# Four output banks, low parts last, and the sums of w_out made early: a change to an attention and cosine-FFN kernel

## The chip, the cores and the metric

The kernel runs on one core of a Trainium2 chip. The metric is the device time of one execution in microseconds (us). The names of engines are those of the profile: PE is TensorE (matmuls; PEld its weight loads), DVE is VectorE, ACT is ScalarE, POOL is GpSimd, SP is SyncE, which issues the transfers. SBUF is the memory on the chip that all engines work from, PSUM the one that PE writes its results to (eight banks of 128 x 512 fp32 values), HBM the memory outside.

## The reference

```python
B, H, S, D = q.shape                       # 8, 8, 576, 64
scores = scale * np.matmul(q, k.transpose(0, 1, 3, 2))
# heads 0-3: the last 32 positions; heads 4-7: every 32nd position
scores = np.where(masks[None], scores, -1e9)
attn = softmax(scores)
x = matmul(attn, v).transpose(0, 2, 1, 3).reshape(B * S, H * D)   # 4608 x 512
h = x @ w_in                               # 512 x 2048
g = h * np.cos(h)
return g @ w_out                           # 2048 x 512
```

## The kernel before, in words

All products of the FFN are made from split operands: a value is the sum of a high part `hi` (rounded to the form that PE multiplies at full rate) and a low part `lo`, and one product takes three matmuls, hi·hi, hi·lo and lo·hi. `split` makes the two parts: a cast (L172, on ACT unless told otherwise) and a subtraction (L173, on POOL unless told otherwise).

**Stage 1** (to about 491 us) runs over 8 batches. For each it makes the attention of the next batch and `h` of this one, in 8 column tiles f of 7 slots each (a batch is 56 slots, `PER_BATCH`; `STEP` is 7). `Block.product` (L524) makes one of seven products of a 2x2 scheme, which needs seven block products in place of eight; `SLOTS` says in which slots they stand. h goes to HBM (`h_all`). Beside the products a plan of slots puts in other work step by step (`in_steps`): the preparation of `w_in`, of `w_out` (`whole_output_weights`, written to `w_all` in HBM in the middle batches; `output_weights` loads and splits a row block n of 16, twelve in the last batch and the last `LATE` = 4 in stage 2), and of sums of blocks of `w_out` that the 2x2 scheme needs (`output_sums`: three sets, for f in `SEVEN` = 1, 3, 5; the sums are made on DVE in the last batch and split there).

**Stage 2** runs over 18 token blocks s (256 tokens) and, in each, over 8 tiles f (two row blocks of w_out, so 256 of the 2048 columns of h). `gate(s, f)` makes g of one tile in steps, and `ahead` issues these steps 6, 4, 3 and 2 tiles before the tile's matmuls (`LEADS`):

- load `h_in` from HBM (L623, five buffers),
- `r`: an int32 rounding of h/2π on ACT (L630), then r = h − 2π·k on DVE (L631, a SCALAR_TENSOR_TENSOR, "stt"; three buffers),
- `wave`: the sine on ACT (L634) into one of three PSUM banks of the pool `sg`,
- in plain tiles: wave·h on DVE (L641), cast to `g_hi` on ACT (L172), `g_lo` by L173, on DVE for f = 2 and 4 (`BY_VECTOR`) and on POOL for 0, 6 and 7,
- in "seven" tiles (f = 1, 3, 5 of the blocks 1 to 16): wave·h into `g` on DVE (L648), three sums on POOL (L649, L650, L653), the cast of 128 x 896 on ACT, and `g_lo` of 128 x 896 on POOL. `g_hi` and `g_lo` have three buffers.

`Outputs.pair` makes the matmuls of a tile (L681): a plain tile takes 12 of 512 columns, a seven tile 21 of 256 columns. They add up in PSUM over the eight tiles of a block in the banks "lower" and "upper" (rows 0 to 127 and 128 to 255 of the block; one pool of three banks) and, for products that both halves share, "more" (two banks). `shared` adds the "more" parts up after f = 5 (ACT L706; DVE L707, L709, L712), and `store` adds them to both halves (DVE L721, twice), or, in blocks 0 and 17, which have no seven tiles, copies them (ACT L727, DVE L725), and stores the rows (L728). PSUM in stage 2 is thus 3 banks of wave, 3 of lower/upper and 2 of "more".

The order of the instructions on each engine isn't the order of the code. A scheduler sets it before the run from a timeline of its own (`schedule_with_timeline_sim=True`); only the matmuls keep the written order (`in_turn`). Any edit in buffers or engines may change the order on ACT, DVE and POOL.

Of the kernel before, what the change touches and what calls it, by code (L numbers as in the profile page):

```python
# [13 lines left out]
F32 = mybir.dt.float32  # L14
# [68 lines left out]

BY_VECTOR = (2, 4)

SUMMED = (14, 28, 35)
LATE = 4

OUTPUTS = (
    (0, "b11", "more", 0), (2, "b21", "upper", 0), (6, "b22", "upper", 1), (1, 3, "lower", 0), (5, 2, "more", 1),  # L90
# [5 lines left out]
def attention_cos_ffn(ctx, tc, qkl, vl, qkvs, w_in, w_out, eye, eye16, mask_l0, mask_l, mask_s, out):  # L96
# [74 lines left out]
    def split(x, hi, lo, cast=nc.scalar.copy, rest=nc.gpsimd):  # L171
        with_product(cast(out=hi, in_=x))  # L172
        rest.tensor_tensor(out=lo, in0=x, in1=hi.bitcast(F32), op=ALU.subtract)  # L173
# [401 lines left out]
        nc.sync.dma_start(out=w_all[n], in_=t)  # L575
        yield

    def output_weights(both, n):
        t = wp.tile([P, 2, 2, 2 * P], F32R, name="w", bufs=2 * NF).rearrange("p l m n -> p l (m n)")
        nc.sync.dma_start(out=both, in_=w_all[n])  # L580
        yield
        split(both, t[:, 0], t[:, 1], nc.vector.tensor_copy)
        wo.append((t[:, 0], t[:, 1]))
        yield

    def whole_tile(cv):
        return cv.tile([P, 512, 2], I32, name="raw", bufs=3).bitcast(F32).rearrange("p n w -> p (n w)")

    def output_sums(cv, n):

        f = SEVEN[n]
        both = whole_tile(cv).rearrange("p (f n) -> p f n", f=2)
        nc.sync.dma_start(out=both, in_=w_all[2 * f:2 * f + 2].rearrange("f p n -> p f n"))
        yield
        b = both.rearrange("p f (j n) -> p (f j) n", j=2)
        t = whole_tile(cv).rearrange("p (j n) -> p j n", j=4)
        first = nc.vector.tensor_tensor(
            out=t[:, :2], in0=b[:, 1:2].broadcast_to([P, 2, 2 * P]), in1=b[:, 0:4:3], op=ALU.subtract
        )
        with_product(first)  # L600
        nc.vector.tensor_tensor(out=t[:, 2], in0=b[:, 3], in1=t[:, 0], op=ALU.subtract)
        nc.vector.tensor_tensor(out=t[:, 3], in0=b[:, 2], in1=t[:, 2], op=ALU.subtract)
        most = wp.tile([P, 2, 3, 2 * P], F32R, name="v")
        sums[f] = [(most[:, 0, n], most[:, 1, n]) for n in range(3)]
        yield
        split(t[:, :3], most[:, 0], most[:, 1], nc.vector.tensor_copy)
        yield
        if n % 3 == 0:
            lasts.append(wp.tile([P, 2, 3, 2 * P], F32R, name="v"))
        last = lasts[-1][:, 0, n % 3], lasts[-1][:, 1, n % 3]  # L610
        split(t[:, 3], *last, nc.vector.tensor_copy)
        sums[f].append(last)
        yield

    wo, lasts, gates, sums = [], [], {}, {}
# [1 line left out]
    def seven(s, f):  # L617
        return 0 < s < NTB - 1 and f in SEVEN
# [49 lines left out]
    class Outputs:  # L668


        def __init__(self, s):
            self.s, self.banks, self.begun = s, {}, set()

        def add(self, name, begin, end, pairs):
            if name not in self.banks:
                n = 4 if name == "more" else 2
                self.banks[name] = pools[name].tile([P, n, 2 * P], F32, name="q")
            at = self.banks[name][:, begin:end].rearrange("p n d -> p (n d)")
            bank = name, begin // 2
            for a, w in pairs:  # L680
                in_turn(nc.tensor.matmul(  # L681
                    at, a, w, start=bank not in self.begun, stop=True, skip_group_check=True
                ))
                self.begun.add(bank)

        def pair(self, f, g_hi, g_lo):
            (b1h, b1l), (b2h, b2l) = wo[2 * f:2 * f + 2]
            if not seven(self.s, f):
                for half, name in enumerate(("lower", "upper")):
                    for n, (wh, wl) in enumerate(((b1h, b1l), (b2h, b2l))):  # L690
                        gh, gl = (g[:, (2 * n + half) * P:(2 * n + half + 1) * P] for g in (g_hi, g_lo))
                        self.add(name, 0, 2, ((gh, wh), (gh, wl), (gl, wh)))
                return
            left, right = slice(0, 2 * P), slice(2 * P, 4 * P)
            plain = {"b11": (b1h[:, left], b1l[:, left]), "b21": (b2h[:, left], b2l[:, left]),
                     "b22": (b2h[:, right], b2l[:, right])}
            for n, w, name, at in OUTPUTS:
                wh, wl = plain[w] if w in plain else sums[f][w]
                gh, gl = (g[:, n * P:(n + 1) * P] for g in (g_hi, g_lo))
                self.add(name, at, at + 1, ((gh, wh), (gh, wl), (gl, wh)))  # L700

        def shared(self):

# [11 lines left out]
        def store(self):  # L715

            rows = out[self.s * TB:(self.s + 1) * TB, :].rearrange("(h p) d -> h p d", h=2)
            for half, name in enumerate(("lower", "upper")):
                o = op.tile([P, 2, 2 * P], F32, name="o", bufs=4)
                if "more" in self.banks:  # L720
                    nc.vector.tensor_tensor(  # L721
                        out=o, in0=self.banks[name], in1=self.t[:, 2 - 2 * half:4 - 2 * half], op=ALU.add
                    )
                elif half:
                    nc.vector.tensor_copy(out=o, in_=self.banks[name])  # L725
                else:
                    nc.scalar.copy(out=o, in_=self.banks[name])  # L727
                nc.sync.dma_start(out=rows[half], in_=o.rearrange("p n d -> p (n d)"))  # L728

# [3 lines left out]
    with ExitStack() as phase:  # L733
# [67 lines left out]
                plan[STEP * f + slot] = partial(first.products, slot)  # L801
        for i, (b, f) in enumerate(itertools.product(range(1, B), range(NF)), NF):
            block = Block(b, f)
            for n, slot in enumerate(SLOTS):
                plan[STEP * i + slot] = partial(block.product, n)
        steps = {}

        def in_steps(work, *slots):
            work = iter(work)
            for slot in slots:  # L810
                steps.setdefault(slot, []).append(partial(next, work, None))
# [9 lines left out]
            in_steps(whole_output_weights(cv, n), at - 10, at)  # L821
        for n in range(NFC - LATE):
            at = (B - 1) * PER_BATCH + STEP * (n // 2) + 12 + 3 * (n % 2)
            in_steps(output_weights(whole_tile(cv)[:, :DM], n), at - 6, at)
        for n, at in enumerate(SUMMED):
            at += (B - 1) * PER_BATCH
            in_steps(output_sums(cv, n), at - 8, at, at + 2, at + 7)
# [36 lines left out]
    pools = {  # L864
        name: ctx.enter_context(
            tc.tile_pool(name=f"ps_{bufs}", bufs=bufs, space=bass.MemoryType.PSUM, reuse_waits="tile")
        ) for name, bufs in (("lower", 3), ("more", 1))
    }
    pools["upper"] = pools["lower"]
    made = {}  # L870
    for n in range(NFC - LATE, NFC):
        weights = output_weights(tp.tile([P, DM], F32, name=f"both{n}"), n)
        next(weights)
        made[n + LATE - NFC + 1] = [weights]
    for i, (s, f) in enumerate(tiles):
        if f == 0:
            block = Outputs(s)
# [105 lines left out]
```

## Time and profile before

| | |
|---|---|
| median of 3 runs | 891.18 us (890.71 to 891.97) |
| the profiled execution | 893.41 us, of which the span of the profile 891.6 us |
| mean granted clock of PE | 0.996 |
| PE busy | 867.6 us, 97% |
| DVE, ACT, POOL busy | 611.6, 506.3, 516.3 us |
| stage 2 | 18 blocks from 491.1 us on; last matmul ends at 887.7 us |

The profile shows one execution by instruction. A row of the timeline has the start, the duration, the engine, the line of the code, the operation, output <- inputs, the shape, a count, and in brackets how long the engine stood idle before it and what released it. A row of the costliest groups has busy time, mean ns of one, then idle time before them and its releaser. Durations in the sums below are those of the profiled execution; what is worked out in them is set against its own time.

### The profile page before, as it was taken

What the parts mean: (1) busy time and instruction counts of PE and PEld (TensorE: products, weight loads), DVE (VectorE), ACT (ScalarE), POOL (GpSimd) and SP (SyncE); (2) the same over time, 40 slices, a digit from 0 to 9 for tenths busy, and PEclk for the clock granted to TensorE, in tenths of its full rate; (3) what the DMA queues carried; (4) which work ended last, traced back from release to release, by engine and by line L of the source; (5) the groups of instructions that cost most, each with busy time, mean ns of one, the idle gap of its engine ahead of it and who ended that gap; (6) DMA issues with size and microseconds to landing.
All of it is one profiled execution on the core that took longest, in us unless ns stands there. A gap on an engine that the chain in (4) does not pass through costs nothing.

```text
span 891.6 us, 22375 instructions
## 1 busy us (share of the span) xinstructions
PE 867.6 (97%) x8871; PEld 788.7 (88%) x8871; DVE 611.6 (69%) x1097; ACT 506.3 (57%) x1004; POOL 516.3 (58%) x455
## 2 busy tenths in 40 slices
PE   8999999999999999999998999999999999999998
PEld 5799899999999998999998888888888888888886
DVE  5688656766676575575459777777777777777772
ACT  4666444435444463453425676666666666666672
POOL 3578974316024151150456787777777777777752
PEclk9899999999999999999999999999999999999999
DMA  9588444565556556544376533344343444433330
GB/s 330 187 286 277 135 150 157 193 224 190 196 185 229 187 196 212 193 162 169 111 233 207 162 115 119 122 124 123 122 123 121 122 123 124 123 124 119 119 99 31
DMA packets 89768, 145.46 MB, mean 163 GB/s; under 512 B 8256, under 2 KB 52544, under 8 KB 89664
## 3 DMA queue, kind: packets, MB, share of 16 engines
q1 hardware_dynamic: 88944, 143.82, 49.5%
q8 instruction: 69, 1.13, 0.5%
q14 instruction: 35, 0.29, 0.1%
q10 hardware_dynamic: 720, 0.23, 0.1%
HBM read 92.63 MB, written 51.38 MB: 162 GB/s over the span
## 4 chain that ended last, share of the span: by engine, by line
PE 37%; DVE 9%; issue 4%; ACT 3%; POOL 3%; POOLq 0%; DVEq 0%
PE q L681 28%; PE m L524 5%; DVE r L631 3%; POOL g_lo L173 3%; PE n L524 3%; ACT r L630 2%; PE o L524 1%; DVE t L709 1%; DVE o L721 1%; ACT wave L634 1%; DVE g L648 1%; DVE t L707 1%; DVE t L712 1%; DVE h L542 0%; PE acc L325 0%
## 5 line engine op out<-in xcount | busy, mean ns | idle before, releaser
L681 PE MATMUL q<-w,g_hi 128*128 128x512 f32 (+1 forms) x1056 | 293.4, 363 | 8.1 <-DVE o L721 8.1
L681 PEld LDWEIGHTS q<-w,g_hi 128*128 128x128 f32 x1056 | 187.6, 189 | 44.9 <-DVE o L721 14.8
L681 PE MATMUL q<-w,g_lo 128*128 128x512 f32 (+1 forms) x528 | 190.3, 360 | 0.0
L631 DVE SCALAR_TENSOR_TENSOR r<-r,h_in 128x512 f32<-128x512 int32 x144 | 144.0, 1019 | 9.8 <-ACT r L630 9.8
L173 POOL TENSOR_TENSOR g_lo<-g,g_hi 128x896 fp32r<-128x896 f32 x48 | 102.1, 2127 | 41.7 <-ACT g_hi L172 41.7
L634 ACT ACTIVATE wave<-r,quarter 128x512 f32<-128x512 f32 x144 | 98.2, 690 | 40.0 <-DVE r L631 40.0
L681 PEld LDWEIGHTS q<-w,g_lo 128*128 128x128 f32 x528 | 99.5, 188 | 15.8 <-POOL g_lo L173 0.2
L524 PE MATMUL m<-x_hi,w 128*128 128x288 f32 x448 | 109.9, 300 | 3.0 <-DVE h L542 2.6
L524 PE MATMUL m<-x_hi,v 128*128 128x288 f32 x448 | 109.0, 298 | 1.2 <-ACT m L532 1.2
L173 POOL TENSOR_TENSOR g_lo<-r,g_hi 128x512 fp32r<-128x512 f32 x60 | 85.8, 1431 | 35.8 <-ACT g_hi L172 34.5
L630 ACT ACTIVATE r<-h_in 128x512 int32<-128x512 f32 x144 | 86.4, 623 | 13.0 <-POOL g_lo L173 12.4
L172 ACT CAST g_hi<-g 128x896 fp32r<-128x896 f32 x48 | 45.3, 944 | 68.8 <-POOL g L653 68.8
L524 PEld LDWEIGHTS m<-x_hi,w 128*128 128x128 f32 x448 | 78.0, 188 | 5.2 <-DVE h L542 3.6
L532 ACT COPY m<-m 128x288 f32<-128x288 f32 x112 | 44.6, 399 | 63.4 <-PE m L524 57.9
L524 PEld LDWEIGHTS m<-x_hi,v 128*128 128x128 f32 x448 | 78.0, 188 | 2.5 <-ACT m L532 1.6
L277 POOL TENSOR_TENSOR pn_s<-e_sb,z 128x324 f32<-128x324 f32 x28 | 21.2, 758 | 94.1 <-DVE z L275 76.3
L277 POOL TENSOR_TENSOR e_sb<-e_sb,z 128x384 f32<-128x384 f32 x24 | 21.0, 873 | 92.6 <-DVE z L275 83.5
L681 PE MATMUL q<-v,g_hi 128*128 128x256 f32 x384 | 71.2, 283 | 0.0
L641 DVE TENSOR_TENSOR r<-wave,h_in 128x512 f32<-128x512 f32 x60 | 41.1, 686 | 39.4 <-ACT wave L634 39.4
L524 PE MATMUL m<-x_lo,w 128*128 128x288 f32 x224 | 66.1, 295 | 0.0
L524 PE MATMUL m<-x_lo,v 128*128 128x288 f32 x224 | 66.1, 295 | 0.0
L648 DVE TENSOR_TENSOR g<-wave,h_in 128x512 f32<-128x512 f32 x48 | 33.1, 689 | 42.3 <-ACT wave L634 42.3
(134 smaller groups left out, 2086.8 us busy)
## 6 DMA issues: line engine op xcount, KB each, us to landing
h_all<-h SPq DMA_DIRECT2D x128, 288.0 KB, 2.7
h_in<-h_all SPq DMA_DIRECT2D x144, 256.0 KB, 2.8
out<-o SPq DMA_DIRECT2D x36, 256.0 KB, 2.1
qk<-in_qkvs SPq DMA_DIRECT2D x28, 324.0 KB, 4.2
qk<-in_qkl SPq DMA_DIRECT2D x21, 416.0 KB, 4.0
raw<-in_w_in SPq DMA_DIRECT2D x16, 512.0 KB, 5.0
raw<-in_w_out SPq DMA_DIRECT2D x16, 512.0 KB, 4.3
v<-in_vl SPq DMA_DIRECT2D x24, 224.0 KB, 3.8
```

The costliest lines, as they stand in the source:

```text
L172: with_product(cast(out=hi, in_=x))
L173: rest.tensor_tensor(out=lo, in0=x, in1=hi.bitcast(F32), op=ALU.subtract)
L277: nc.gpsimd.tensor_tensor(out=pn, in0=e, in1=z[:, :n].unsqueeze(2).broadcast_to([P, n, w]), op=ALU.mult)
L524: in_turn(nc.tensor.matmul(bank, a[:, c * P:(c + 1) * P], y[:, c], start=first and i == 0, stop=i == len(ops) - 1, skip_group_check=True,))
L532: nc.scalar.copy(out=t, in_=self.bank[name[0]])
L630: with_product(nc.scalar.activation(out=k, in_=h, func=AF.Copy, scale=1.0 / (2.0 * math.pi), bias=0.25))
L631: nc.vector.scalar_tensor_tensor(out=r, in0=k, scalar=-2.0 * math.pi, in1=h, op0=ALU.mult, op1=ALU.add)
L634: sin = nc.scalar.activation(out=wave, in_=r, func=AF.Sin, bias=quarter)
L641: nc.vector.tensor_tensor(out=low, in0=wave, in1=h, op=ALU.mult)
L648: nc.vector.tensor_tensor(out=g[:, :4].rearrange("p n t -> p (n t)"), in0=wave, in1=h, op=ALU.mult)
L681: in_turn(nc.tensor.matmul(at, a, w, start=bank not in self.begun, stop=True, skip_group_check=True))
L707: nc.vector.tensor_tensor(out=self.t[:, 4], in0=more[:, 1], in1=self.t[:, 0], op=ALU.add)
```

## The change

1. PSUM: "lower" and "upper" share four banks instead of three; `wave` has two instead of three.
2. `Outputs.pair` issues, for a tile, first all matmuls with the high part of g and then all with its low part. In the very last tile the products of the upper half are made in two halves of 256 columns, and `store` copies and stores that half in two parts.
3. `output_sums` moves from the last batch to the middle batches (slots 2·56 + 17·(2f + 2) and 8 later), from DVE to POOL, and stores its sums in a new HBM tensor `t_all`. `split_sums` loads a set and splits it: two sets in the last batch, the third in tiles 6 and 7 of stage 2; their casts are on ACT and not on DVE.
4. `output_weights`: the casts of the ten row blocks in the last batch are on ACT and not on DVE; six row blocks instead of four are prepared in stage 2 (`LATE`), their casts on ACT and DVE in turn.
5. The very last tile of stage 1 has the seven products in other slots (`LAST`).

```diff
+LAST = (0, 4, 2, 3, 7, 6, 8)
...
-SUMMED = (14, 28, 35)
-LATE = 4
+SUMMED = (14, 28)
+LATE = 6
...
+    t_all = dram.tile([len(SEVEN), P, 2 * DM], F32, name="t_all")
...
-    def output_weights(both, n):
+    def output_weights(room, n, cast):
+        both = room()
...
-        split(both, t[:, 0], t[:, 1], nc.vector.tensor_copy)
+        split(both, t[:, 0], t[:, 1], cast)
...
-        first = nc.vector.tensor_tensor(
+        with_product(nc.gpsimd.tensor_tensor(
             out=t[:, :2], in0=b[:, 1:2].broadcast_to([P, 2, 2 * P]), in1=b[:, 0:4:3], op=ALU.subtract
-        )
-        with_product(first)
-        nc.vector.tensor_tensor(out=t[:, 2], in0=b[:, 3], in1=t[:, 0], op=ALU.subtract)
-        nc.vector.tensor_tensor(out=t[:, 3], in0=b[:, 2], in1=t[:, 2], op=ALU.subtract)
+        ))
+        nc.gpsimd.tensor_tensor(out=t[:, 2], in0=b[:, 3], in1=t[:, 0], op=ALU.subtract)
+        nc.gpsimd.tensor_tensor(out=t[:, 3], in0=b[:, 2], in1=t[:, 2], op=ALU.subtract)
+        nc.sync.dma_start(out=t_all[n], in_=t.rearrange("p j n -> p (j n)"))
+        yield
+
+    def split_sums(room, n):
+        t = room()
+        nc.sync.dma_start(out=t, in_=t_all[n])
+        yield
+        t = t.rearrange("p (j n) -> p j n", j=4)
         most = wp.tile([P, 2, 3, 2 * P], F32R, name="v")
...
-        split(t[:, :3], most[:, 0], most[:, 1], nc.vector.tensor_copy)
+        split(t[:, :3], most[:, 0], most[:, 1])
...
-            for a, w in pairs:
-                in_turn(nc.tensor.matmul(
-                    at, a, w, start=bank not in self.begun, stop=True, skip_group_check=True
-                ))
-                self.begun.add(bank)
...
+            for group in groups:
+                for n, both, to in group:
+                    for w in both:
+                        self.add(*to, g_hi[:, n * P:(n + 1) * P], w)
+                for n, (w, _), to in group:
+                    self.add(*to, g_lo[:, n * P:(n + 1) * P], w)
...
+                parts = (slice(0, 1), slice(1, 2)) if self.last and half else (slice(0, 2),)
+                for i, part in enumerate(parts):
+                    if "more" not in self.banks:
+                        copy = nc.scalar.copy if half == i else nc.vector.tensor_copy
+                        copy(out=o[:, part], in_=self.banks[name][:, part])
...
-                        name="sg", bufs=3, space=bass.MemoryType.PSUM, side="right", reuse_waits="tile"
+                        name="sg", bufs=2, space=bass.MemoryType.PSUM, side="right", reuse_waits="tile"
...
-        ) for name, bufs in (("lower", 3), ("more", 1))
+        ) for name, bufs in (("lower", 4), ("more", 1))
```

In the new file the lines of the gate are: r L642 (was L630), stt L643 (L631), sine L646 (L634), wave·h L653 (L641) and L660 (L648), POOL's three sums L661, L662, L665 (L649, L650, L653), cast L176 (L172), subtraction L177 (L173), matmul L692 (L681), `shared` L728 to L734 (L706 to L712), the two sums of `store` L743 (L721).

The edits also give another order on the engines of the gate. On POOL, one steady block (token block 6; `g` is a seven tile's, in turn f = 1, 3, 5; `g_lo<-r` is the low part of a plain tile, f = 6, 7 of block 5 and then f = 0), before:

```order
L173 TENSOR_TENSOR g_lo_9251<-g_9228,g_hi_9250 128x896
L173 TENSOR_TENSOR g_lo_9284<-r_9233,g_hi_9283 128x512
L173 TENSOR_TENSOR g_lo_9308<-r_9257,g_hi_9307 128x512
L649 TENSOR_TENSOR g_9349<-g_9349 128x128
L650 TENSOR_TENSOR g_9349<-g_9349 128x256
L173 TENSOR_TENSOR g_lo_9344<-r_9290,g_hi_9343 128x512
L653 TENSOR_TENSOR g_9349<-g_9349 128x128
L649 TENSOR_TENSOR g_9409<-g_9409 128x128
L173 TENSOR_TENSOR g_lo_9374<-g_9349,g_hi_9373 128x896
L650 TENSOR_TENSOR g_9409<-g_9409 128x256
L653 TENSOR_TENSOR g_9409<-g_9409 128x128
L173 TENSOR_TENSOR g_lo_9434<-g_9409,g_hi_9433 128x896
```

The same place after, from the low part of f = 0 on (the three low parts ahead of it stand as before):

```order
L177 TENSOR_TENSOR g_lo_9354<-r_9300,g_hi_9353 128x512
L661 TENSOR_TENSOR g_9359<-g_9359 128x128
L662 TENSOR_TENSOR g_9359<-g_9359 128x256
L665 TENSOR_TENSOR g_9359<-g_9359 128x128
L177 TENSOR_TENSOR g_lo_9384<-g_9359,g_hi_9383 128x896
L661 TENSOR_TENSOR g_9419<-g_9419 128x128
L662 TENSOR_TENSOR g_9419<-g_9419 128x256
L665 TENSOR_TENSOR g_9419<-g_9419 128x128
L661 TENSOR_TENSOR g_9483<-g_9483 128x128
L177 TENSOR_TENSOR g_lo_9444<-g_9419,g_hi_9443 128x896
L662 TENSOR_TENSOR g_9483<-g_9483 128x256
L665 TENSOR_TENSOR g_9483<-g_9483 128x128
```

The low part of f = 0 now stands ahead of all three sums of f = 1 (before, behind the second), and the first sum of f = 5 (L661, `g_9483`) ahead of the low part of f = 3 (before, behind it).

On DVE in the same block, from the stt of f = 1 on, before:

```order
L631 SCALAR_TENSOR_TENSOR r_9314<-r_9314,h_in_9260 128x512
L648 TENSOR_TENSOR g_9349<-wave_9347,h_in_9260 128x512
L631 SCALAR_TENSOR_TENSOR r_9354<-r_9354,h_in_9293 128x512
L631 SCALAR_TENSOR_TENSOR r_9380<-r_9380,h_in_9317 128x512
...
L631 SCALAR_TENSOR_TENSOR r_9414<-r_9414,h_in_9357 128x512
L721 TENSOR_TENSOR o_9397<-q_9174,t_9340 128x512
L721 TENSOR_TENSOR o_9400<-q_9181,t_9340 128x512
L173 TENSOR_TENSOR g_lo_9404<-wave_9377,g_hi_9403 128x512
L641 TENSOR_TENSOR wave_9437<-wave_9437,h_in_9357 128x512
L631 SCALAR_TENSOR_TENSOR r_9440<-r_9440,h_in_9383 128x512
L648 TENSOR_TENSOR g_9473<-wave_9471,h_in_9383 128x512
```

And after:

```order
L643 SCALAR_TENSOR_TENSOR r_9324<-r_9324,h_in_9270 128x512
L643 SCALAR_TENSOR_TENSOR r_9364<-r_9364,h_in_9303 128x512
L660 TENSOR_TENSOR g_9359<-wave_9357,h_in_9270 128x512
...
L643 SCALAR_TENSOR_TENSOR r_9450<-r_9450,h_in_9393 128x512
L743 TENSOR_TENSOR o_9407<-q_9184,t_9350 128x512
L743 TENSOR_TENSOR o_9410<-q_9189,t_9350 128x512
L177 TENSOR_TENSOR g_lo_9414<-wave_9387,g_hi_9413 128x512
L653 TENSOR_TENSOR wave_9447<-wave_9447,h_in_9367 128x512
L643 SCALAR_TENSOR_TENSOR r_9488<-r_9488,h_in_9427 128x512
L660 TENSOR_TENSOR g_9483<-wave_9481,h_in_9393 128x512
```

The stt of f = 2 (`r_9364`) moved ahead of the product of f = 1 (L660), and the stt of f = 5 (`r_9450`) ahead of the two sums of `store`; that of f = 6 (`r_9488`) ahead of the product of f = 5.

On PE, the tile f = 0 of block 6 (two weights each for the lower and the upper bank), before and after:

```order
L681 MATMUL q_9419<-w_7380,g_hi_9343 128x512 x2
L681 MATMUL q_9419<-w_7380,g_lo_9344 128x512
L681 MATMUL q_9419<-w_7410,g_hi_9343 128x512 x2
L681 MATMUL q_9419<-w_7410,g_lo_9344 128x512
L681 MATMUL q_9426<-w_7380,g_hi_9343 128x512 x2
L681 MATMUL q_9426<-w_7380,g_lo_9344 128x512
```
```order
L692 MATMUL q_9429<-w_7391,g_hi_9353 128x512 x2
L692 MATMUL q_9429<-w_7422,g_hi_9353 128x512 x2
L692 MATMUL q_9434<-w_7391,g_hi_9353 128x512 x2
L692 MATMUL q_9434<-w_7422,g_hi_9353 128x512 x2
L692 MATMUL q_9429<-w_7391,g_lo_9354 128x512
L692 MATMUL q_9429<-w_7422,g_lo_9354 128x512
```

The first use of the low part moved from the third matmul to the ninth.

More of the change, by code (lines that the diff above doesn't have):

```diff
@@ L596, in output_sums @@
         t = whole_tile(cv).rearrange("p (j n) -> p j n", j=4)
-        first = nc.vector.tensor_tensor(
+        with_product(nc.gpsimd.tensor_tensor(
             out=t[:, :2], in0=b[:, 1:2].broadcast_to([P, 2, 2 * P]), in1=b[:, 0:4:3], op=ALU.subtract
-        )
-        with_product(first)
-        nc.vector.tensor_tensor(out=t[:, 2], in0=b[:, 3], in1=t[:, 0], op=ALU.subtract)
-        nc.vector.tensor_tensor(out=t[:, 3], in0=b[:, 2], in1=t[:, 2], op=ALU.subtract)
+        ))
[8 more added lines that the diff above has]
+        t = t.rearrange("p (j n) -> p j n", j=4)
         most = wp.tile([P, 2, 3, 2 * P], F32R, name="v")
-        sums[f] = [(most[:, 0, n], most[:, 1, n]) for n in range(3)]
-        yield
-        split(t[:, :3], most[:, 0], most[:, 1], nc.vector.tensor_copy)
+        split(t[:, :3], most[:, 0], most[:, 1])
+        sums[SEVEN[n]] = [(most[:, 0, n], most[:, 1, n]) for n in range(3)]
         yield
@@ L610, in output_sums @@
         last = lasts[-1][:, 0, n % 3], lasts[-1][:, 1, n % 3]
-        split(t[:, 3], *last, nc.vector.tensor_copy)
-        sums[f].append(last)
+        split(t[:, 3], *last)
+        sums[SEVEN[n]].append(last)
         yield
@@ L671, in __init__, with add @@
         def __init__(self, s):
-            self.s, self.banks, self.begun = s, {}, set()
-        def add(self, name, begin, end, pairs):
+            self.s, self.banks, self.begun, self.last = s, {}, set(), s == NTB - 1
+        def add(self, name, begin, end, a, w):
             if name not in self.banks:
@@ L679, in add @@
             bank = name, begin // 2
-            for a, w in pairs:
-                in_turn(nc.tensor.matmul(
-                    at, a, w, start=bank not in self.begun, stop=True, skip_group_check=True
-                ))
-                self.begun.add(bank)
-        def pair(self, f, g_hi, g_lo):
[L687 to L700, printed above, removed]
@@ new lines, in add @@
+            in_turn(nc.tensor.matmul(at, a, w, start=bank not in self.begun, stop=True, skip_group_check=True))
+            self.begun.add(bank)
+        def pair(self, f, g_hi, g_lo):
+            w1, w2 = wo[2 * f:2 * f + 2]
+            if seven(self.s, f):
+                left, right = slice(0, 2 * P), slice(2 * P, 4 * P)
+                plain = {name: [w[:, part] for w in both] for name, both, part in (
+                    ("b11", w1, left), ("b21", w2, left), ("b22", w2, right),
+                )}
+                products = [
+                    (n, plain[w] if w in plain else sums[f][w], (name, at, at + 1)) for n, w, name, at in OUTPUTS
+                ]
+            else:
+                products = [
+                    (2 * n + half, w, (name, 0, 2)) for half, name in enumerate(("lower", "upper"))
+                    for n, w in enumerate((w1, w2))
+                ]
+            groups = [products]
+            if self.last and f == NF - 1:
+                groups = [products[:2], *(
+                    [(n, [w[:, 2 * P * i:2 * P * (i + 1)] for w in both], ("upper", i, i + 1))
+                     for n, both, _ in products[2:]] for i in range(2)
+                )]
+            for group in groups:
[4 more added lines that the diff above has]
+                    self.add(*to, g_lo[:, n * P:(n + 1) * P], w)
@@ L723, in store @@
                     )
[L724 to L728, printed above, removed]
+                parts = (slice(0, 1), slice(1, 2)) if self.last and half else (slice(0, 2),)
[3 more added lines that the diff above has]
+                        copy(out=o[:, part], in_=self.banks[name][:, part])
+                    nc.sync.dma_start(
+                        out=rows[half].rearrange("p (n d) -> p n d", n=2)[:, part], in_=o[:, part]
+                    )
     wp = ctx.enter_context(tc.tile_pool(name="wp", bufs=NF, reuse_waits="tile"))
@@ L803, in attention_cos_ffn @@
             block = Block(b, f)
-            for n, slot in enumerate(SLOTS):
+            for n, slot in enumerate(LAST if i == B * NF - 1 else SLOTS):
                 plan[STEP * i + slot] = partial(block.product, n)
@@ L823, in attention_cos_ffn @@
             at = (B - 1) * PER_BATCH + STEP * (n // 2) + 12 + 3 * (n % 2)
-            in_steps(output_weights(whole_tile(cv)[:, :DM], n), at - 6, at)
+            in_steps(output_weights(lambda: whole_tile(cv)[:, :DM], n, nc.scalar.copy), at - 6, at)
+        for n, f in enumerate(SEVEN):
+            at = 2 * PER_BATCH + 17 * (2 * f + 2)
+            in_steps(output_sums(cv, n), at, at + 8)
         for n, at in enumerate(SUMMED):
             at += (B - 1) * PER_BATCH
-            in_steps(output_sums(cv, n), at - 8, at, at + 2, at + 7)
+            in_steps(split_sums(lambda: whole_tile(cv), n), at - 6, at, at + 4)
         for b in range(1, B):
@@ L871, in attention_cos_ffn @@
     for n in range(NFC - LATE, NFC):
-        weights = output_weights(tp.tile([P, DM], F32, name=f"both{n}"), n)
+        cast = nc.vector.tensor_copy if n % 2 else nc.scalar.copy
+        weights = output_weights(lambda: tp.tile([P, DM], F32, name="both", bufs=LATE), n, cast)
         next(weights)
-        made[n + LATE - NFC + 1] = [weights]
+        made[n + LATE - NFC] = [weights]
+    for n in range(len(SUMMED), len(SEVEN)):
+        weights = split_sums(lambda: tp.tile([P, 2 * DM], F32, name="t"), n)
+        next(weights)
+        for i in (LATE, LATE + 1):
+            made.setdefault(i, []).append(weights)
     for i, (s, f) in enumerate(tiles):
```

## The prediction

> **What bounds the kernel now.** I read the page first: engine totals, then the costliest groups.
>
> ```profile
> span 891.6 us, 22375 instructions
> PE 867.6 (97%) x8871; PEld 788.7 (88%) x8871; DVE 611.6 (69%) x1097; ACT 506.3 (57%) x1004; POOL 516.3 (58%) x455
> ...
> L681 PE MATMUL q<-w,g_hi 128*128 128x512 f32 (+1 forms) x1056 | 293.4, 363 | 8.1 <-DVE o L721 8.1
> ...
> L631 DVE SCALAR_TENSOR_TENSOR r<-r,h_in 128x512 f32<-128x512 int32 x144 | 144.0, 1019 | 9.8 <-ACT r L630 9.8
> ```
>
> TensorE (PE) is 97% busy, and the one wait of its stage-2 matmuls is for the output copy. Second view, the waits of PE; third, its timeline at two block boundaries.
>
> ```profile
> PE q L681 <- DVE o L721: 8.1, 15, 1.2
> ```
> ```profile
> 601.28 0.39 PE L681 MATMUL q<-w,g_lo 128*128 128x512 f32 x1
> 602.13 0.50 PE L681 MATMUL q<-w,g_hi 128*128 128x512 f32 x1 [0.47 <-DVE o L721]
> ...
> 624.16 0.50 PE L681 MATMUL q<-w,g_hi 128*128 128x512 f32 x1 [0.51 <-DVE o L721]
> ```
>
> The two boundaries stand 624.16 − 602.13 = 22.03 us apart. From 601.28 to 602.13 two starts lie 0.85 us apart; undisturbed they are 0.23 apart, so a boundary costs 0.62 us plus a slower first matmul (0.50 against 0.39), say 0.73 to 0.76. Without that a block would take about 21.27 us. The easy reading is: too few banks, give a fourth, gain some 15 × 0.76 = 11 us.
>
> The fourth view asks who waits for whom around these matmuls.
>
> ```profile
>   DVE o L721: 22.9, 31
> ...
>   ACT g_hi L172: 4.1, 3
>   POOL g_lo L173: 1.3, 1
> ```
>
> The first row is PE's and its loads' wait for the copy. The other two are all that the gate engines ever wait for PE, 5.4 us in four places of 18 blocks. If PE were the bound, the gate would fill its three buffers and wait for PE every block. It doesn't. So the gate loop has a period of 22.03 us by itself, and PE's spare 0.76 us shows at the place where PE is held last. The fifth view is one block of that loop on POOL, DVE and ACT.
>
> ```profile
> 611.94 2.13 POOL L173 TENSOR_TENSOR g_lo<-g,g_hi 128x896 fp32r<-128x896 f32 x1 [1.05 <-ACT g_hi L172]
> 614.03 1.75 POOL L173 TENSOR_TENSOR g_lo<-r,g_hi 128x512 fp32r<-128x512 f32 x1
> 617.03 1.30 POOL L173 TENSOR_TENSOR g_lo<-r,g_hi 128x512 fp32r<-128x512 f32 x1 [1.25 <-ACT g_hi L172]
> 618.70 0.91 POOL L649 TENSOR_TENSOR g<-g 128x128 f32<-128x128 f32 x1 [0.36 <-DVE g L648]
> 619.69 1.07 POOL L650 TENSOR_TENSOR g<-g 128x256 f32<-128x256 f32 x1
> 620.72 1.30 POOL L173 TENSOR_TENSOR g_lo<-r,g_hi 128x512 fp32r<-128x512 f32 x1
> 621.98 0.47 POOL L653 TENSOR_TENSOR g<-g 128x128 f32<-128x128 f32 x1
> ...
> 623.51 2.12 POOL L173 TENSOR_TENSOR g_lo<-g,g_hi 128x896 fp32r<-128x896 f32 x1 [0.55 <-ACT g_hi L172]
> 625.58 0.74 POOL L650 TENSOR_TENSOR g<-g 128x256 f32<-128x256 f32 x1
> ...
> 628.25 2.12 POOL L173 TENSOR_TENSOR g_lo<-g,g_hi 128x896 fp32r<-128x896 f32 x1 [1.05 <-ACT g_hi L172]
> ...
> 633.98 2.13 POOL L173 TENSOR_TENSOR g_lo<-g,g_hi 128x896 fp32r<-128x896 f32 x1 [1.05 <-ACT g_hi L172]
> ```
> ```profile
> 613.10 1.52 DVE L631 SCALAR_TENSOR_TENSOR r<-r,h_in 128x512 f32<-128x512 int32 x1
> ...
> 616.48 0.69 DVE L631 SCALAR_TENSOR_TENSOR r<-r,h_in 128x512 f32<-128x512 int32 x1 [0.41 <-ACT r L630]
> 617.93 0.69 DVE L648 TENSOR_TENSOR g<-wave,h_in 128x512 f32<-128x512 f32 x1 [0.76 <-ACT wave L634]
> ...
> 620.08 0.41 DVE L707 TENSOR_TENSOR t<-q,t 128x256 f32<-128x256 f32 x1
> 620.53 0.69 DVE L709 TENSOR_TENSOR t<-q,t 128x512 f32<-128x512 f32 x1
> ...
> 623.43 1.28 DVE L721 TENSOR_TENSOR o<-q,t 128x512 f32<-128x512 f32 x2
> ```
> ```profile
> 615.81 0.63 ACT L630 ACTIVATE r<-h_in 128x512 int32<-128x512 f32 x1 [0.47 <-POOL g_lo L173]
> ...
> 617.20 0.69 ACT L634 ACTIVATE wave<-r,quarter 128x512 f32<-128x512 f32 x1 [0.25 <-DVE r L631]
> ...
> 622.48 0.95 ACT L172 CAST g_hi<-g 128x896 fp32r<-128x896 f32 x1 [0.86 <-POOL g L653]
> ```
>
> Call a tile by its pair number f, the L631 instruction "stt", the seven tiles' three adds p1, p2, p3. The cycle: the low part of f6 ends at 615.78 and frees the buffer for r of f1; ACT r (615.81), stt (616.48), sine (617.20), g (617.93); then POOL p1, p2, the low part of f0 between them, p3; the cast (622.48), the low part of f1 (623.51), and over f3 and f5 (628.25, 633.98) to the next f6. From 611.94 to 633.98 is 22.04 us, and each row starts within 0.1 us of the end of the one before it in this chain.
>
> Two rows in it also show a collision. The stt at 613.10 takes 1.52 us where the free one at 616.48 takes 0.69: it comes while the low part of 611.94 runs (to 614.07), and ends 0.55 us after that. And the low part at 614.03 takes 1.75 where 617.03 takes 1.30: it ends 1.16 after the stt. So an stt and any POOL operation exclude each other; who waits gets the turn at the next hand-over. The mean of all stt, 1019 ns against 690, says that it happens all along. L648, L709 and L721, which have an input in PSUM, stay at 0.64 to 0.69 beside POOL.
>
> The Trainium skill says the same in "SBUF — State Buffer", section "Who interferes with whom": a VectorE instruction with two SBUF inputs contends with a GpSimd instruction that reads SBUF, and whoever issues first has the shared ports for the whole instruction. By this rule the change's order, not its banks, decides; the trace agrees with its 1.52 and 0.69 us.
>
> **The change part by part.**
>
> *Banks and pair order.* L721's wait goes: with four lower/upper banks a block's first matmul finds its bank free. PE's low parts start later in a pair: for 12 matmuls of 0.23 us at the 9th instead of the 3rd, 1.4 us later. That is slack once; it doesn't shorten the gate's cycle, so it is worth nothing per block. With two wave banks instead of three, ACT's sine of f3 to f7 waits for a DVE operation two tiles back; I walked these gates and in the walk none binds longer than 0.1 us except through the order below.
>
> *Order of the gate loop.* The new code gives the scheduler another result: on POOL the low part of f0 stands ahead of p1 of f1, and p1 of f5 ahead of the low part of f3; on DVE stt f2 ahead of g f1, and stt f5 ahead of the two L743 copies and g f5. I walk it with durations from the rows above, zero at the start of f5's low part, engines starting within 0.05 to 0.08 us of their release.
> POOL: low parts f5 0 to 2.1, f6 to 3.4, f7 to 4.65. r f1 3.4 to 4.05; stt f1 asks at 4.1, in f7's low part, and ends at 5.2 (4.65 + 0.55). The low part of f0, behind it, ends at 5.2 + 1.16 = 6.35. stt f2 asks at 5.35, is held by that, and ends at 6.9. Only now g f1, 6.85 to 7.5, and POOL idles from 6.35 to 7.6. p1, p2, p3 of f1 with stt f3 between them: to 9.7. Cast 9.8 to 10.7, low part of f1 10.8 to 12.9.
> DVE meanwhile: L729, stt f3, L731, mul f2, stt f4, L734, g f3 in steps of 0.6 (0.35 for 256 columns); stt f5 asks at 11.2, 0.4 us after the low part of f1 has begun, and ends at 13.45. Behind it the L743 pair (1.28, as at 623.43), the low part of f2, mul f4, stt f6; g f5 16.4 to 17.1. POOL finished p3 of f3 at 15.1 and now waits for g f5, since p1 of f5 stands ahead of the low part of f3: 17.2 to 17.65. The low part of f3, from 17.7, is held by stt f7 and ends at 20.2; p2, p3 of f5 to 21.7; cast 0.95; the next f5 starts at 22.7 to 23.0, by the size of the hand-overs.
> The same bookkeeping over the old order gives 22.05 to 22.3, where the rows give 22.04. The difference is +0.55 to +0.95 a block; I take +0.75, period 22.8. The loop runs from the first row below to the second, 15 periods: 15 × 0.75 = **+11.3** (+8.2 to +14.3).
>
> ```profile
> 523.87 2.13 POOL L173 TENSOR_TENSOR g_lo<-g,g_hi 128x896 fp32r<-128x896 f32 x1 [1.05 <-ACT g_hi L172]
> ...
> 854.15 2.13 POOL L173 TENSOR_TENSOR g_lo<-g,g_hi 128x896 fp32r<-128x896 f32 x1 [1.05 <-ACT g_hi L172]
> ```
>
> *Drain.* From 856.28 (end of the second row) to the last matmul before was 31.3 us, with one 1.46 us boundary in it. After: the low parts of f5 (7 × 0.12 = 0.84, begun up to 0.5 late), f6 and f7 (24 × 0.227 = 5.45), block 17 (96 × 0.227 = 21.8, +0.15 for its halves): 28.7. **−2.5** (−3.0 to −1.5).
>
> *Last batch.* The weights' casts go from DVE to ACT, a third of the sums' preparation goes to stage 2, LAST puts two other products between the last "m" product and its copy. Three waits of PE stood there, two of them:
>
> ```profile
> 483.99 0.40 PE L524 MATMUL n<-x_hi,w 128*128 128x288 f32 x1 [1.11 <-DVE h L542]
> ...
> 490.16 0.40 PE L524 MATMUL m<-x_hi,w 128*128 128x288 f32 x1 [1.49 <-DVE h L542]
> ```
>
> 1.11 + 1.49 and restarts, about 3. If all goes and the first gates start as much earlier: **−3.2** (0 if ACT becomes late instead, −4.5 if the first two blocks gain too).
>
> *Middle batches.* Nine POOL instructions for the sums, three of them 128x512, and three stores. The nearest rows:
>
> ```profile
> L199 POOL TENSOR_TENSOR sums<-v 128x256 f32<-128x256 f32 x8 | 5.9, 741 | 0.4
> ```
> ```profile
> POOL e_sb L277 <- DVE z L275: 83.5, 19, 10.5
> ```
>
> 3 × (1.3 + 2 × 0.74) = 8.3 us of POOL where it idles 83.5 us for DVE; what covers them is that idle time. If they land ahead of an urgent low part, each set costs up to 1.5: 0 to +4.5, or a little below 0 since DVE loses that work. **+0.5**. The stores queue on SP behind POOL's sums, with loads due long after; nothing.
>
> *Tail.* The upper half of block 17 is copied in two, so that after the last matmul a 256-column copy on ACT and a 128 KB store remain, where there was this:
>
> ```profile
> 887.77 0.69 DVE L725 COPY o<-q 128x512 f32<-128x512 f32 x1 [12.58 <-PE q L681]
> ```
>
> A copy of half the columns takes about 0.36 to 0.41 (as L707): **−0.35** (−0.8 to +0.2).
>
> Sum: 11.3 − 2.5 − 3.2 + 0.5 − 0.35 = +5.75. The profiled execution took 893.41 us, its span and 1.8 around it, and is 2.2 above the median of the runs, 891.18; so 899.2 for such an execution and **897** for a median.
>
> **The rivals.**
>
> *PE is the bound after all (other side).* The fourth bank ends the boundary wait and the late low parts let the gate lag, so blocks take 21.27: 15 × −0.76 = −11.4, with the other terms −5.55: 891.18 − 17 = 874. For it: 97% busy and a wait for one bank at each boundary. Against it: the gate engines' 5.4 us of waits for PE. It decides if the gate's period falls under 21.27; in the walk, stt f5 asking 0.4 us earlier, ahead of the low part of f1, would bring it to about 21.5, still not under. The Trainium skill gives the general form in "Perfetto Trace Analysis", section "Optimization Strategy": consistent bubbles can mean that there isn't enough SBUF or PSUM for the next tile. By that sentence 874 would be right; this trace agrees as to the bubble, not as to its cause.
>
> *One collision fails to happen.* If stt f2 slips ahead of f0's low part, or stt f7 misses that of f3, the period is 22.0 to 22.4: 15 × (0 to 0.36) − 5.55 gives 885.6 to 891. For it: the margins in the walk are 0.7 and 0.3 us, and the walk is good to 0.2.
>
> *A further wait.* ACT, with six more casts in the first block and the gates of two wave banks, becomes late, or the sums block POOL in the middle: over 904.
>
> **How the numbers follow.** The gate loop at 22.6 to 23.0: 0.65, with own range 891 to 904 (8.2 or 14.3 for the loop, other terms −8 to −1). PE bound: 0.15, 874. One collision less: 0.13. Worse: 0.07. The range leaves out the PE-bound case and some of the worst: 881 to 903. A measurement of this kernel tells about 0.2%, 1.8 us (its runs spread 890.71 to 891.97). Faster: the PE-bound case and most of the third, 0.27. Same: the rest of it and the foot of the likeliest, 0.07. Slower 0.66.
>
> **What would show it.** In the changed profile: boundaries 22.8 us apart; no wait of PE for L743, but a wait of 1 to 1.5 us per block for POOL's low part of f3 (L177); the mean of L643 above 1019 ns; POOL idle ahead of L661 for g, twice a block; no wait for L542's counterpart at 484 and 490. Wrong I am if PE shows no wait in stage 2 (then the gate had slack that I denied), or if the stt of f5 is seen to end before the low part of f1 starts.

## The result, and the profile after

The changed kernel takes 900.58 us (median, 899.1 to 900.8) against 891.58 for the kernel before, measured beside it: 1.0099 times as long, with a 95% interval of 1.0081 to 1.0116. The forecast was 897, between 881 and 903.

The page of the changed kernel, its span, totals and the groups that answer to those of before:

```profile
span 898.7 us, 22488 instructions
PE 865.6 (96%) x8877; PEld 789.8 (88%) x8877; DVE 607.6 (68%) x1069; ACT 518.0 (58%) x1024; POOL 517.2 (58%) x464
...
L643 DVE SCALAR_TENSOR_TENSOR r<-r,h_in 128x512 f32<-128x512 int32 x144 | 160.3, 1115 | 49.3 <-ACT r L642 49.2
...
L692 PE MATMUL q<-w,g_lo 128*128 128x512 f32 (+1 forms) x530 | 129.7, 362 | 19.6 <-POOL g_lo L177 19.6
...
L661 POOL TENSOR_TENSOR g<-g 128x128 f32<-128x128 f32 x48 | 29.8, 622 | 48.3 <-DVE g L660 48.3
```

PE's 8.1 us of waits for the output copy are gone, and in their place stand 19.6 us of waits for the low parts that POOL makes. The stt's mean rose from 1019 to 1115 ns, and POOL's idle time ahead of its first sum from 6.8 us (then L649) to 48.3. PE's work was the same but for six matmuls (products of the last tile are made in halves); it waited more.

The timeline of the changed kernel, one block of POOL, then DVE in the same block (start, duration, what ran, idle time before it):

```profile
608.34 0.46 POOL L661 TENSOR_TENSOR g<-g 128x128 f32<-128x128 f32 x1 [1.98 <-DVE g L660]
608.75 2.55 POOL L177 TENSOR_TENSOR g_lo<-g,g_hi 128x896 fp32r<-128x896 f32 x1
...
613.91 2.13 POOL L177 TENSOR_TENSOR g_lo<-g,g_hi 128x896 fp32r<-128x896 f32 x1 [1.05 <-ACT g_hi L176]
616.00 4.25 POOL L177 TENSOR_TENSOR g_lo<-r,g_hi 128x512 fp32r<-128x512 f32 x3
621.48 0.46 POOL L661 TENSOR_TENSOR g<-g 128x128 f32<-128x128 f32 x1 [1.23 <-DVE g L660]
...
624.68 2.13 POOL L177 TENSOR_TENSOR g_lo<-g,g_hi 128x896 fp32r<-128x896 f32 x1 [1.05 <-ACT g_hi L176]
...
631.03 0.47 POOL L661 TENSOR_TENSOR g<-g 128x128 f32<-128x128 f32 x1 [1.98 <-DVE g L660]
631.46 2.55 POOL L177 TENSOR_TENSOR g_lo<-g,g_hi 128x896 fp32r<-128x896 f32 x1
```
```profile
619.25 1.55 DVE L643 SCALAR_TENSOR_TENSOR r<-r,h_in 128x512 f32<-128x512 int32 x1 [0.15 <-ACT r L642]
620.72 0.68 DVE L660 TENSOR_TENSOR g<-wave,h_in 128x512 f32<-128x512 f32 x1
...
625.14 2.22 DVE L643 SCALAR_TENSOR_TENSOR r<-r,h_in 128x512 f32<-128x512 int32 x1
627.28 1.28 DVE L743 TENSOR_TENSOR o<-q,t 128x512 f32<-128x512 f32 x2
...
630.28 0.68 DVE L660 TENSOR_TENSOR g<-wave,h_in 128x512 f32<-128x512 f32 x1
```

Set zero at 613.91, the start of f5's low part, and the forecast's walk can be read off. The stt of f2 (619.25) was held until the low part of f0 had ended, so g of f1 starts at 620.72, 6.81 after zero (walk: 6.85). The low part of f1 starts at 10.77 (10.8). The stt of f5 (625.14, 11.23; walk 11.2) comes 0.46 us after it, takes 2.22 us, where a free one takes 0.68 (623.61 in the same timeline), and ends at 13.45 (13.45). The two sums of `store` and the rest queue behind it; g of f5 starts at 16.37 (16.4). POOL has stood idle for 1.98 us by 631.03, since its next instruction needs g of f5, and only then makes the low part of f3 (17.55; walk 17.7). From 608.75 to 631.46 is 22.71 us. PE's timeline shows the other side, one wait a block, within f3's pair, and nothing at the boundary:

```profile
611.36 0.62 PE L692 MATMUL q<-w,g_lo 128*128 128x256 f32 x3 [1.23 <-POOL g_lo L177]
```

### The profile page after: what moved, and what is told of

Read it like the earlier page. It is cut to its first block, busy times and chain, and to the rows that moved or that the text cites. A ratio compares the mean times of both kernels' runs of the same rounds, so it can differ in the third digit from the quotient of the medians.

```text
span 898.7 us, 22488 instructions
## 1 busy us (share of the span) xinstructions
PE 865.6 (96%) x8877; PEld 789.8 (88%) x8877; DVE 607.6 (68%) x1069; ACT 518.0 (58%) x1024; POOL 517.2 (58%) x464
## 4 chain that ended last, share of the span: by engine, by line
PE 52%; POOL 24%; issue 11%; ACT 6%; DVE 5%; DMA 2%; SPq 0%; POOLq 0%; ACTq 0%; DVEq 0%
PE m L528 19%; POOL g_lo L177 15%; PE n L528 10%; PE q L692 6%; PE m L499 5%; PE o L528 4%; ACT r L642 3%; POOL g L662 3%; POOL g L661 2%; PE acc L329 2%; PE acc L394 2%; POOL g L665 2%; PE acc L311 1%; DVE r L643 1%; ACT g_hi L176 1%
## 5 line engine op out<-in xcount | busy, mean ns | idle before, releaser
L692 PE MATMUL q<-w,g_hi 128*128 128x512 f32 (+1 forms) x1060 | 233.5, 360 | 1.5 <-ACT g_hi L176 1.5
L692 PEld LDWEIGHTS q<-w,g_hi 128*128 128x128 f32 x1060 | 182.2, 189 | 32.9 <-ACT g_hi L176 2.0
L643 DVE SCALAR_TENSOR_TENSOR r<-r,h_in 128x512 f32<-128x512 int32 x144 | 160.3, 1115 | 49.3 <-ACT r L642 49.2
L692 PE MATMUL q<-w,g_lo 128*128 128x512 f32 (+1 forms) x530 | 129.7, 362 | 19.6 <-POOL g_lo L177 19.6
L646 ACT ACTIVATE wave<-r,quarter 128x512 f32<-128x512 f32 x144 | 99.5, 691 | 65.9 <-DVE g_lo L177 48.0
L177 POOL TENSOR_TENSOR g_lo<-g,g_hi 128x896 fp32r<-128x896 f32 x48 | 108.8, 2266 | 34.1 <-ACT g_hi L176 34.1
L692 PEld LDWEIGHTS q<-w,g_lo 128*128 128x128 f32 x530 | 92.8, 189 | 37.7 <-POOL g_lo L177 22.8
L642 ACT ACTIVATE r<-h_in 128x512 int32<-128x512 f32 x144 | 89.5, 623 | 35.0 <-POOL g_lo L177 32.9
L177 POOL TENSOR_TENSOR g_lo<-r,g_hi 128x512 fp32r<-128x512 f32 x60 | 84.2, 1417 | 19.1 <-ACT g_hi L176 17.0
L653 DVE TENSOR_TENSOR r<-wave,h_in 128x512 f32<-128x512 f32 x60 | 41.1, 685 | 43.2 <-ACT wave L646 43.2
L176 ACT CAST g_hi<-g 128x896 fp32r<-128x896 f32 x48 | 44.9, 936 | 26.4 <-POOL g L665 26.4
L661 POOL TENSOR_TENSOR g<-g 128x128 f32<-128x128 f32 x48 | 29.8, 622 | 48.3 <-DVE g L660 48.3
L528 PE MATMUL n<-x_hi,v 128*128 128x288 f32 x224 | 55.2, 301 | 1.8 <-ACT n L536 1.8
```

What stands on the lines that cost most here:

```text
L528: in_turn(nc.tensor.matmul(bank, a[:, c * P:(c + 1) * P], y[:, c], start=first and i == 0, stop=i == len(ops) - 1, skip_group_check=True,))
L642: with_product(nc.scalar.activation(out=k, in_=h, func=AF.Copy, scale=1.0 / (2.0 * math.pi), bias=0.25))
L643: nc.vector.scalar_tensor_tensor(out=r, in0=k, scalar=-2.0 * math.pi, in1=h, op0=ALU.mult, op1=ALU.add)
L646: sin = nc.scalar.activation(out=wave, in_=r, func=AF.Sin, bias=quarter)
L653: nc.vector.tensor_tensor(out=low, in0=wave, in1=h, op=ALU.mult)
L661: pool.tensor_tensor(out=g[:, 4], in0=g[:, 0], in1=g[:, 2], op=ALU.add)
```

## The experiments

"The walk" in the expectations is the forecast's bookkeeping, taken over the order of the kernel in question: fixed durations from rows, engines in their order, stt and POOL exclusive. Its values for the kernels before and after (22.08 and 22.73 us) were worked out when both profiles were known, so only those for the new kernels are forecasts. Three theories stood against each other. A: the order of the gate loop and its collisions set the period. B: the two wave banks hold the sine. C: the low parts, used later, let PE hold the gate's buffers longer.

### One instruction put back in its place

`order(later, first)` only fixes which of two instructions on the same engine is issued first. The edit, beside the changed kernel:

```diff
+    rules = [(('stt', 5), ('o', 1))]
...
+        for later, first in rules:
+            if later == (kind, f) and 1 < s < NTB - 1:
+                order(ins, marked[first[0], s, first[1]], "as before")
```

> The changed kernel with one thing more: in the blocks 2 to 16 the stt of f5 on DVE is put behind the first of the two sums of store (as it stood before). Nothing else is asked of the order; banks, pairs, sums stay as changed. Theory A (collisions set the gate loop, and stt f5 held by the low part of f1 delays g f5, for which POOL waits): the walk over the new order gives 21.98 us a block against 22.73 for the changed kernel, so 15 x -0.7 = -10.6 and about 890 us. Theory B (two wave banks instead of three hold the sine, and that sets 22.7): the banks are still two, so 22.7 and 900.6 us stay. Theory C (the third reading: the low parts stand later in a pair, PE frees the gate's buffers later): 900.6 too.

Measured: 890.68 us against 890.99, ratio 0.9998 (0.9989 to 1.0007). One edge on DVE, in 15 blocks, took back all of the loss. The rule names the sum of the upper half, the second of the two; in the trace the stt of f5 stands behind both. By the traces nothing else moved: by operation and tile, POOL and ACT run from the first instruction to the last in the order of the changed kernel, and DVE differs in these 15 places alone. The timeline of DVE, then of POOL:

```profile
604.44 0.68 DVE L670 TENSOR_TENSOR g<-wave,h_in 128x512 f32<-128x512 f32 x1
...
622.58 1.27 DVE L753 TENSOR_TENSOR o<-q,t 128x512 f32<-128x512 f32 x2
623.77 1.03 DVE L652 SCALAR_TENSOR_TENSOR r<-r,h_in 128x512 f32<-128x512 int32 x1
```
```profile
600.03 2.14 POOL L177 TENSOR_TENSOR g_lo<-g,g_hi 128x896 fp32r<-128x896 f32 x1 [1.06 <-ACT g_hi L176]
...
605.20 0.46 POOL L671 TENSOR_TENSOR g<-g 128x128 f32<-128x128 f32 x1 [0.36 <-PE q L702]
...
622.12 2.13 POOL L177 TENSOR_TENSOR g_lo<-g,g_hi 128x896 fp32r<-128x896 f32 x1 [1.05 <-ACT g_hi L176]
```

The sums of `store` run during the low part of f1, which they don't disturb, and the stt of f5 comes after them, and takes 1.03 us instead of 2.22. POOL waits 0.36 us, not 1.98, ahead of f5's first sum. (The row names PE as the releaser, but it starts 0.08 us after the product of f5, which it reads, has ended: 604.44 + 0.68 in DVE's timeline.) The period is 22.09 us (600.03 to 622.12; the walk said 21.98). That is still 0.07 us above the 22.02 of the kernel before, so with this one put back the other moved instructions cost the loop next to nothing. Theories B and C fall for the changed kernel: banks and pairs were the same here. C has a number of its own against it: in all of the changed kernel ACT and POOL wait 3.2 us, in two places, for the matmuls of the gate's buffers. The view of waits shows how B could have misled:

```profile
ACT wave L656 <- DVE g_lo L177: 51.8, 32, 1.9
```

The sine waits 51.8 us in this kernel for a bank that DVE holds, more than the 48.0 us in the slower one. It is idle time of an engine with time to spare: with the same two banks the loop is back at 22.09 us.

### POOL's half of the chain

The same edit with another edge, `(('p1', 5), ('lo', 3))`. Here DVE and ACT keep the order of the changed kernel, and POOL differs in 15 places, one in each block.

> The changed kernel with one thing more: POOL's first sum of f5 is put behind the low part of f3, as it stood before; the stt of f5 stays ahead of the sums of store. Theory A: stt f5 is still held by the low part of f1, but POOL no longer waits for g f5 ahead of the low part of f3: the walk gives 22.36 us a block against 22.73, so 15 x -0.37 = -5.5, about 895 us. If the place of stt f5 is all that counts: 900.6.

Measured: 894.87 us against 891.45, ratio 1.0043 (1.0028 to 1.0058); period 22.37. So the loss needs both moves: with the stt of f5 held as before, 0.35 of the 0.70 us a block come back when POOL has the low part of f3 to do meanwhile. And one of the forecast's signs is shown to be no measure:

```profile
L652 DVE SCALAR_TENSOR_TENSOR r<-r,h_in 128x512 f32<-128x512 int32 x144 | 175.2, 1218 | 47.8 <-ACT r L651 47.2
```

The mean of the stt is 1218 ns here, above the changed kernel's 1115, in a kernel that is 6 us faster. What counts is who waits behind the held one.

### The collisions taken away

ACT writes the rounded integer into the wave's PSUM bank, so that the stt has one input in PSUM:

```diff
-        k = r.bitcast(I32)
+        wave = sg.tile([P, 2 * TB], F32, name="wave")
+        k = wave.bitcast(I32)
...
-        wave = sg.tile([P, 2 * TB], F32, name="wave")
         sin = nc.scalar.activation(out=wave, in_=r, func=AF.Sin, bias=quarter)
```

This edit changes the scheduler's order on all three engines too. On the changed kernel:

> The changed kernel, but ACT writes the rounded integer of r into the wave's PSUM bank and not into the r buffer, so that the stt reads one input from PSUM and one from SBUF; the wave's bank is taken two steps earlier. The order on the engines comes out another. Theory A: an stt with a PSUM input doesn't exclude POOL, stt takes 0.69 us on average in place of 1.12, the gate's period falls under PE's 21.2 to 21.3, PE is the bound: 15 x -1.45 = -22, so 874 to 880 us. Theory B (the two wave banks are the limit): each bank is now held longer, so slower, over 905 us. Theory C: no change.

Measured: 875.66 us against 890.99, ratio 0.9825 (0.9808 to 0.9841). And on the kernel before, with nothing of the change:

> The kernel before with the rounded integer of r in the wave's PSUM bank, as in e2, and nothing of the change: three lower/upper and three wave banks. Theory A: no collisions of stt and POOL, the gate's period falls under PE's, the walk gives 21.2 us a block and an end 13 us earlier: 876 to 880 us. If the boundary wait for a bank is real by itself, once the gate is fast, PE still loses 0.75 us a block: 22.0, about 889.

Measured: 876.7 us against 891.45, ratio 0.9839 (0.9824 to 0.9854). The stt on the page, first of the changed kernel with this edit, then of the kernel before with it:

```profile
L653 DVE SCALAR_TENSOR_TENSOR r<-wave,h_in 128x512 f32<-128x512 int32 x144 | 98.7, 687 | 54.0 <-POOL g_lo L177 32.6
```
```profile
L641 DVE SCALAR_TENSOR_TENSOR r<-wave,h_in 128x512 f32<-128x512 int32 x144 | 96.7, 682 | 4.7 <-POOL g_lo L173 2.7
```

687 and 682 ns, and 695 at most: no stt is held any more. In both kernels PE's blocks start 21.22 us apart, which is PE's own time: its matmuls wait 0.7 us for the gate in all of stage 2 of the first, and never in the second. The second kernel also answers whether the fourth bank was ever needed: it has three. Its view of PE's matmuls lists who waited for them:

```profile
  ACT g_hi L172: 97.4, 104
  DVE o L735: 16.9, 2
  ACT o L737: 7.0, 2
  DVE o L731: 5.6, 14
```

No idle time stands before PE's matmuls in this view, and the gate's cast waits 97.4 us for PE, 104 times. This is what a kernel looks like whose bound is PE; in the kernel before it was 4.1 us in 3 times. The boundary wait went without a fourth bank. With this edit the rest of the change is worth little: 0.9825 and 0.9839 have overlapping intervals.

### Parts of the change alone

The matmul order alone, on the kernel before:

> The kernel before with the matmuls of a pair in the new order (all high parts, then all low parts) and nothing else of the change; three banks each. Theory A: the scheduler answers with another order on DVE and POOL, for which the walk gives 22.94 us a block against 22.08: 15 x 0.86 = +13, 903 to 907 us, though the edit moves only matmuls. Theory B: three wave banks, so no loss: 889 to 892. Theory C: a loss, but from PE's buffers, with waits of ACT or POOL for PE in every block.

Measured: 906.88 us, ratio 1.0174 (1.0159 to 1.0189), period 22.87. An edit that only puts the same matmuls in another order made the kernel 16 us slower, according to the walk through the order that the scheduler then gave DVE and POOL (22.94 us a block; no run put that order back). Theory C would have ACT and POOL wait for PE in every block; they do so in four places each:

```profile
  POOL g_lo L173: 10.6, 4
...
  ACT g_hi L172: 5.4, 4
```

In PE's waits, with three banks, the loss reads once more like a lack of banks:

```profile
PE q L680 <- DVE o L726: 21.4, 15, 2.6
```

The banks alone, on the kernel before:

> The kernel before with four lower/upper banks and two wave banks, and nothing else of the change. Easy reading (a bank was lacking): PE's wait at the boundaries goes, 15 x -0.76 = -11, about 880 us. Theory A (the gate loop has the period): the walk over its order gives 22.20 us a block against 22.08, so 15 x 0.12 = +2 and 891 to 894, and PE's wait goes from the output copy to the gate's operands.

Measured: 891.68 us, ratio 1.0005 (0.9994 to 1.0016), period 22.14. The wait moved, to the tenth of a microsecond:

```profile
PE q L681 <- POOL g_lo L173: 8.1, 15, 0.6
```

Before, it read 8.1 us, 15 times, for the output copy. The fourth bank does what it says and in sum is worth nothing here, because the operands come no sooner: the loop loses 15 × 0.12 us, and the end, from the low part of f5 in block 16 to the last matmul, gains 1.65 (29.81 against 31.46).

The banks undone, on the changed kernel:

> The changed kernel with three lower/upper and three wave banks as before; low parts last and the early sums stay. The scheduler's order comes out another. Theory A: by the walk over that order 21.97 us a block, so 15 x -0.7 = -10.8 and 889 to 892 us, and stt f5 is not held for 2 us any more. Theory B: also about 22.0 and 890, but with the wait of the sine for DVE gone as the cause. Theory C: stays 900.

Measured: 896.82 us, ratio 1.0063 (1.0048 to 1.0078), against the 889 to 892 expected: a miss of 5 us above the range. The sign was right, and the size was not. The period was 22.28 on average, not 21.97: 22.23 in the steady blocks, and 23.23 for the first. PE's waits, and then who waited for PE's matmuls, show what the walk leaves out:

```profile
PE q L692 <- DVE o L743: 12.4, 15, 1.6
PE q L692 <- DVE o L750: 3.4, 1, 3.4
```
```profile
  ACT g_hi L176: 37.9, 35
  POOL g_lo L177: 28.0, 18
```

With three banks PE is held at each boundary (12.4 us) and once at the first (3.4), so it is further behind the gate at the end: from the low part of f5 in block 16 to the last matmul it takes 32.7 us, 28.96 in the changed kernel. And here the gate does wait for PE, 53 times, where in the changed kernel it did twice: PE, held at the boundary, gives the gate's buffers back late, as theory C had it, and the walk has no PE in it. That this makes the 0.26 us by which a steady block is longer than the walk has it is read from the waits; no run tried it. It suggests that with the low parts last the fourth bank is worth something: with it, and one edge on DVE, the kernel took 890.68 us (the order on the engines is another, so this is no clean comparison).

### The head start that was lost

`LATE = 4` in the changed kernel:

> The changed kernel with LATE = 4: four row blocks of w_out in stage 2 and not six. The steady order stays the changed kernel's by the walk, 22.73 us a block. Theory A for the lost head start (POOL has two more subtractions of 1.3 us and those of the third set of sums, 2.6 us, between the gates of block 0): from the first matmul of stage 2 to the end of the low part of f5 in block 1 it is 38.97 us in the changed kernel and 34.93 in the kernel before; here 1.6 to 2.6 us less than 38.97, and 898 to 899.5 us if the last batch doesn't pay for it. If the head start is lost to the two wave banks or to the order, it stays 39.0 and 900.6.

Measured: 898.69 us, ratio 1.0086 (1.0071 to 1.0101); from the first matmul of stage 2 to the end of the low part of f5 in block 1 it is 37.22 us against 38.97. POOL in block 0, first in the changed kernel, then here:

```profile
494.39 4.52 POOL L177 TENSOR_TENSOR w<-both,w 128x512 fp32r<-128x512 f32 x3
...
503.26 1.85 POOL L177 TENSOR_TENSOR v<-t,v 128x768 fp32r<-128x768 f32 x1
...
506.78 0.74 POOL L177 TENSOR_TENSOR v<-t,v 128x256 fp32r<-128x256 f32 x1
507.48 1.74 POOL L177 TENSOR_TENSOR g_lo<-r,g_hi 128x512 fp32r<-128x512 f32 x1
```
```profile
494.82 3.28 POOL L177 TENSOR_TENSOR w<-both,w 128x512 fp32r<-128x512 f32 x2
```

The two row blocks that went back to stage 1 bring back 1.75 us of the 4.04 lost. The runs shown above speak against the other explanations: with the banks alone this stretch takes 34.78 us and with the matmul order alone 34.70, against 34.93 in the kernel before, and the changed kernel with the banks undone still takes 38.26. That the third set of sums (1.85 + 0.74) accounts for the other 2.3 us is argued from its rows, not tried.

## Why the prediction was right, and where it was off

All against the two profiled spans, 898.7 − 891.6 = +7.1:

| step | forecast | measured |
|---|---|---|
| start of the kernel (no part of the change) | 0 | −2.1 |
| middle batches | +0.5 | +1.0 |
| last batch | −3.2 | −3.7 |
| first two blocks of stage 2 | 0 | +4.0 |
| gate loop, 15 blocks | +11.3 | +10.6 |
| drain | −2.5 | −2.5 |
| tail | −0.35 | −0.2 |

The −2.1 us arose within the first 60 us of the execution. The profiled execution of before took longer there than every other one of this case (they reach the same matmul 1.2 to 2.7 us earlier, with parts of the change or without), so it is no effect of the change; without it the sum is +9.2, and the medians differ by 9.0.

- The main step, that the gate loop and not PE has the period, and that the new order makes it longer, is shown: by the walk's times in the rows, by the one edge that took all back, and by the two kernels without collisions. Of the signs named, the blocks (22.7 us apart), PE's wait (1.23 us in each block for the low part of f3) and POOL's two idle times in each block (1.23 and 1.98 us) came true.
- The rival with PE as the bound (874 us) was refuted for this change, and is what the kernel does once the collisions are gone: 875.66. The evidence that decided against it was the right one, who waits for PE. The rival with one collision less did not occur either: both that it names happened (the stt of f2 took 1.55 us, the low part of f3 2.55 instead of 2.13).
- The step that failed: "If all goes and the first gates start as much earlier" (last batch). PE did start stage 2 earlier, by 4.83 us of which 3.7 came from the last batch, but the gates of blocks 0 and 1 did not follow, since more preparation had been moved onto POOL there (shown for 1.75 of the 4.0 us, argued for the rest). The forecast counted the moved casts on ACT and DVE and left out the subtractions on POOL that go with each of them, two of 1.3 us and a set of sums of 2.6. It had named the place in the third rival, but with the wrong engine. These 4 us are nearly all of the difference between 897 and 900.58.
- The sign "mean of L643 above 1019 ns" came true, and means nothing by itself (1218 ns in a faster kernel).

## What to carry to other kernels

When the busiest engine waits at the same place in every block, ask whether anybody waits for it: if the engines that feed it never do, they have the period, and a buffer at that place only moves the wait. If they do wait, as with three banks and late low parts above, the buffer may count. Then walk one period of the feeding loop with durations from the trace; where a scheduler sets the order, walk the order that it gives after the edit, since an edit in banks or in matmuls may move an instruction on another engine that costs more than the edit could bring. When work is moved, count each of its instructions on each engine, the cheap followers too.

## What was not expected of the hardware

With its integer input in PSUM, the stt took 682 to 687 ns on average beside the same POOL instructions, against 1019 to 1218 with both inputs in SBUF, and ACT's rounding took no longer when it wrote to PSUM (589 to 597 ns against 623): one input moved from SBUF to PSUM, with the order that the scheduler then gave, was worth 14.8 us (876.7 against 891.45). The hand-over between a held stt and POOL was as regular as the durations, and the same in both directions: the held one ends at the end of the one that held it, plus its own free time, less 0.14 us (0.55 = 0.69 − 0.14 for the stt, 1.16 = 1.30 − 0.14 for a low part of 512 columns). Walks with these gave the periods of 22.09, 22.37, 22.72, 22.87 and 22.14 us within 0.11 us; the one miss, by 0.3, is the kernel with three banks in place of four and all else of the change, where the gate also waits for PE.
